# VectorE for one tile's output copies, the sums of w_out in one place, and sixteen small products of zeros: a change to a fused RWKV-6 and GELU-MLP kernel

## The chip, the cores and the metric

The kernel runs on one core of a Trainium2 chip. Its time is the device time in microseconds (us). Of a profiled execution there is also the span: the time from the core's first to its last instruction.

The engines are TensorE (matrix products; PE in the profile, PEld for its weight loads), VectorE (DVE), ScalarE (ACT), GpSimd (POOL) and SyncE (SP), which here only issues DMAs. A product of fp32 operands is executed as two passes, so the profile counts two matrix products for one in the code.

## The reference

The reference is a linear attention with a state (RWKV-6), followed by an MLP with exact GELU. All arrays are fp32 except the two weight matrices, which arrive as 64-bit floats.

```python
# r, k, v, w: (4, 8, 768, 48); u: (8, 48)
for t in range(S):
    cur = einsum('bhd,bhe->bhde', u[None] * kt, vt)
    y[:, :, t] = einsum('bhd,bhde->bhe', rt, state + cur)
    state = wt[:, :, :, None] * state + einsum('bhd,bhe->bhde', kt, vt)
x = y.transpose(0, 2, 1, 3).reshape(3072, 384)
h = x @ w_in                                   # w_in: (384, 2048)
g = 0.5 * h * (1.0 + erf(h / sqrt(2)))
out = g @ w_out                                # w_out: (2048, 384)
```

## The kernel before

The 3072 tokens are cut into eight tiles x = 0 to 7 of T = 384 tokens, two for each batch element. For each tile, `attention(x, unit)` computes the attention output, transposed, into the tile's `xT`, and `mlp(x)` computes the tile's rows of the output. Both are generators. The body of each `yield` is a piece of work, called a slot (attention) or a step (MLP) here. Each engine executes its instructions strictly in the order in which the generators emit them, so the order is written out by hand: the last loop of the kernel walks through the steps of `mlp(x - 1)` and, after chosen steps, emits slots of `attention(x)` and the first two slots of `attention(x + 1)`.

**The prelude.** A VectorE instruction fills `zeros` (bf16). `keep_warm(n)` issues n products of zeros of 512 columns into a PSUM tile that nobody reads (L194). Eight of them stand ahead of everything on TensorE, and two or three more stand after each slot of the first tile. The first tile's attention is done in two units of half the heads each, slot by slot. In the slots, TensorE makes products into the PSUM tile `d` (L406), VectorE scales r and k in place (L451) and copies the parts of `d` under a mask into `a_sb` (L461, L417). Slots that follow use transposes (L581), products of k and v (`kv_ps`, L607), the states (L622), and the products that give `y_ps` (L648, L689).

**The first MLP, `mlp(0)`.** It has steps 0 to 33. In steps 0 to 15, TensorE multiplies `xT` by w_in into `h_ps` (L886), and ScalarE applies GELU, the last 128 tokens going to `alone` (L889, L891). In steps 16 to 31 the products of the first 256 tokens with w_out are summed in two PSUM tiles `o_ps` (L974); at step 31 ScalarE copies both to SBUF (L979) and SP stores them (L794). Steps 32 and 33 are the two halves of the sum over the last 128 tokens (L900): the first goes to SBUF with a ScalarE copy (L990), the second is added to it by VectorE (L993). All of these sums and `h_ps` share two PSUM banks, tag "mm": a tile waits until the one two before it has been read.

Beside these steps, up to step 24, VectorE and ScalarE convert the weights from 64-bit floats (L295 to L314, `convert`), and the second tile's attention proceeds. Its last slot (at step 30) has the products L689, the ScalarE copy L715, six small DMAs out of it (L719, four on SP and two on ScalarE's queue) and six ScalarE copies into `xT` (L712).

**The sums of w_out, `w_sums`.** From the second tile on, the MLP replaces eight block products by seven, with sums and differences of blocks. The sums of w_out's blocks are made once: eight VectorE instructions of 128 x 768 elements (L739), one for each `next(more)`. In the kernel before, four are emitted at steps 30 to 33 of `mlp(0)`, and four at steps 9 to 12 of `mlp(1)`. `make_quarter_masks` issues nine small VectorE instructions (L246 to L260) and five GpSimd ones (L250, L255).

**Attention from the third tile on.** Slot one is four VectorE products (L356) and a transposing sum (L343). Slot two is the products of w (L375), more products and sums (L350, L379, L343). Then come rows laid out by ScalarE and VectorE (L502, L507, L508), the products L522 and L529 on TensorE, the updates of r and k (L536, L542, L545), the masked copies (L560, L567), and a block transpose of k (L481) whose off-diagonal blocks are moved by DMA (L476) and whose diagonal ones by ScalarE (L591). The products L607 need all these blocks. `place` and `place_next` list the steps after which slots are emitted.

Of the kernel before, what the change touches and what calls it, by code (L numbers as in the profile page):

```python
# [44 lines left out]
def kernel(  # L45
# [25 lines left out]
    nc = tc.nc  # L71
# [7 lines left out]
    NF = DF // 128  # L79
# [54 lines left out]
    def load(x, dma):  # L134

        if x >= NX:
            return
        loaded[x] = [None, None]
        for i in range(3):
            if i == 1:  # L140
                load_v(x, dma)
                yield
            t = bufs[x % 2 if i == 0 else 1]
            for j in range(3):
                a = i * ALL + j * ALL // 3
                dma.dma_start(out=t[:, a:a + ALL // 3], in_=rkw[x, :, a:a + ALL // 3])
                yield
# [33 lines left out]
    zeros = const.tile([128, BANK], BF16, name="zeros")  # L181
# [3 lines left out]

    nc.scalar.activation(out=zeros[:, 0:1], in_=zeros[:, 0:1], func=AF.Gelu)

    def keep_warm(n, elsewhere=False):
        if elsewhere:
            t = pd.tile([128, 2, BANK], F32, name="warm", tag="d")[:, 0]  # L190
        else:
            t = ps.tile([128, BANK], F32, name="warm", tag="mm", bufs=2)
        for _ in range(n):
            nc.tensor.matmul(t, lhsT=zeros[:, 0:128], rhs=zeros, start=True, stop=True)  # L194

    keep_warm(8)


    masks = {h: const.tile([128, C // 2], U8, name=f"mask{h}") for h in LEVELS[:-1]}
# [34 lines left out]
    for i, h in enumerate(QUARTERS):  # L234
        for a in range(3):
            w_q = (3 - a) * C // 4
            z = q_ints[1 if a == 0 else 2]
            o = i * C if a < 2 else i * C + C // 2
# [18 lines left out]
    def make_quarter_masks():  # L257
        make_fine()
        for (h, a), m_q in m_qs.items():
            nc.vector.tensor_tensor(out=quarter[h][a], in0=s_qs[h][:, 0:m_q.shape[1]], in1=m_q, op=ALU.is_equal)  # L260
# [22 lines left out]
    def convert():  # L283
        for _ in conversion():
            pass
# [446 lines left out]
    def w_sums():  # L732

        sums.extend(cv.tile([128, HF, HM], F32, name="t", tag="raw", bufs=AHEAD) for _ in range(4))
        s3_sb.append(cv.tile([128, HF, 128], F32, name="s3", tag="raw", bufs=AHEAD))
        for i, (x, y) in enumerate((((0, 1), (0, 0)), ((1, 1), 0), ((1, 1), (0, 1)), ((1, 0), 1))):
            for k in range(2):
                ks = slice(k * FG, (k + 1) * FG)
                nc.vector.tensor_sub(sums[i][:, ks], w_quarter(*x, k), sums[y][:, ks] if isinstance(y, int) else w_quarter(*y, k))  # L739
                yield  # L740
# [40 lines left out]
    def mlp(x):  # L781
# [8 lines left out]
        def block(a, b, j):  # L790
            return gs[2 * b + j // FG][:, j % FG, a * 128:(a + 1) * 128]

        def store(row0, o_sb, c0=0):
            nc.sync.dma_start(out=out[row0:row0 + 128, c0:c0 + o_sb.shape[1]], in_=o_sb)  # L794

        def new_sums(tag):
            return cv.tile([128, FG, 128], F32, name="s", tag=tag)
# [83 lines left out]
        for n, group in enumerate(() if final else (0, 2, 1, 3) if halves else range(4)):  # L881
            gs[group] = gp.tile([128, FG, T], F32, name="g")
            for f in range(group * FG, (group + 1) * FG):
                h_ps = ps.tile([128, BANK], F32, name="h_ps", tag="mm", bufs=2)[:, 0:T]
                for j in range(NJ):
                    nc.tensor.matmul(h_ps, lhsT=w_in_sb[:, f // FI, j, f % FI * 128:(f % FI + 1) * 128], rhs=xT[:, j, :],  # L886
                                     start=(j == 0), stop=(j == NJ - 1))
                t = T - 128 if waits else T
# [9 lines left out]
        def product(o, lhs, rhs, start=False):  # L898
            for j in range(HF):
                nc.tensor.matmul(o, lhsT=lhs(j), rhs=rhs(j), start=start and j == 0, stop=(j == HF - 1),  # L900
                                 skip_group_check=True)

        def of_sums(s):
            return lambda j: s[j // FG][:, j % FG, :]

        def of_t(i):
            return lambda j: sums[i][:, j, :]

        def of_blocks(a, b):
            return lambda j: block(a, b, j)  # L910
# [4 lines left out]
        def of_w(b, c):  # L915
            return lambda j: w_out_sb[:, b * HF + j, c * HM:(c + 1) * HM]

        def psum():
            return ps.tile([128, BANK], F32, name="o_ps", tag="mm", bufs=2)[:, 0:HM]

        def two_rows():
            return [wk.tile([128, DM], F32, name="o_sb", bufs=2) for _ in range(2)]
# [3 lines left out]
        if halves:  # L926
            o_sb = two_rows()
            p1, u2, u3 = (wk.tile([128, HM], F32, name=name, bufs=1) for name in ("p1", "u2", "u3"))
            o1, o2 = psum(), psum()
            product(o1, of_blocks(0, 0), of_w(0, 0), True)  # L930
            nc.scalar.copy(out=p1, in_=o1)  # L931
            yield
            product(o2, of_blocks(1, 1), of_t(3), True)
            nc.scalar.copy(out=o_sb[1][:, 0:HM], in_=o2)
            yield
            product(o1, of_blocks(0, 1), of_w(1, 0))
            nc.scalar.copy(out=o_sb[0][:, 0:HM], in_=o1)
            yield
            product(o2, of_sums(s2), of_t(1), True)
            nc.vector.tensor_add(u2, o2, p1)  # L940
            yield
            product(o1, of_sums(s1), of_t(0), True)
            nc.scalar.copy(out=o_sb[1][:, HM:], in_=o1)
            for k in range(2):

                nc.vector.tensor_sub(s2[k], gs[k + 2][:, :, 0:128], s2[k])
            yield
            product(o2, of_sums(s3), of_t(2))
            nc.vector.tensor_add(u3, o2, p1)
            for c in range(2):  # L950
                z = o_sb[1][:, c * HM:(c + 1) * HM]
                nc.vector.tensor_add(z, z, u3)
            store(row0 + 128, o_sb[1])
            if ends:
                s1 = [new_sums("f") for k in range(2)]
                for k in range(2):
                    nc.vector.tensor_add(s1[k], gs[k][:, :, 256:], gs[k + 2][:, :, 256:])
                    nc.vector.tensor_sub(s3[k], alone[:, k * FG:(k + 1) * FG], gs[k][:, :, 256:])
            yield
            product(o1, of_sums(s2), of_w(1, 1))  # L960
            nc.vector.tensor_add(o_sb[0][:, HM:], o1, u2)
            store(row0, o_sb[0])
            if ends:
                s2 = [new_sums("e") for k in range(2)]
                for k in range(2):
                    nc.vector.tensor_sub(s2[k], s1[k], alone[:, k * FG:(k + 1) * FG])
            yield

        else:

            o_ps = [ps.tile([128, BANK], F32, name="o_ps", tag="mm", bufs=2)[:, 0:DM] for _ in range(2)]
            for f in range(NF):
                for i, o in enumerate(o_ps):
                    nc.tensor.matmul(o, lhsT=block(i, f // HF, f % HF), rhs=w_out_sb[:, f, :], start=(f == 0), stop=(f == NF - 1))  # L974
                if f < NF - 1:
                    yield
            for i, o in enumerate(o_ps):
                o_sb = wk.tile([128, DM], F32, name="o_sb", bufs=2)
                nc.scalar.copy(out=o_sb, in_=o)  # L979
                store(row0 + i * 128, o_sb)  # L980
            yield


        if waits:
# [3 lines left out]
            o_sb = wk.tile([128, DM], F32, name="o_sb", bufs=2)  # L988
# [7 lines left out]
        elif ends:  # L996
            o_sb = two_rows()
# [69 lines left out]
    for x in range(1, NX):  # L1067

        place = [1, 3, 5, 7, 9, 11, 13, 15, 18, 20, 26, 30] if x == 1 else [1, 6, 8, 13, 15, 16, 18, 18, 20, 21]
        place_next = [31, 33] if x == 1 else [25, 27] if x % 2 == 0 else [21, 24]  # L1070
        loads = load(x + 1, nc.scalar if x > 1 else nc.sync)

        times = range(18, 28) if x == 1 else (2, 3, 4, 5, 17, 18, 19, 20, 21, 22)
        following = attention(x + 1, 0) if x + 1 < NX else iter(())
        for step, _ in enumerate(mlp(x - 1)):
            if x == 1 and step == 2 * NF - 2:

                make_quarter_masks()
                more = w_sums()

            if x == 1 or step > 8:
                next(more, None)
            if x == 1 and step in (0, 2, 4, 6, 8, 10, 12, 14, 15, 17, 18, 20, 22, 24):
                convert()
            if step in times:
                next(loads, None)
            while place and place[0] <= step:
                place.pop(0)
                next(slots, None)
            while place_next and place_next[0] <= step:  # L1090
                place_next.pop(0)
                next(following, None)
            if x == NX - 1:

                if step == 18:
                    more_h = h_sums()
                for _ in range({18: 1, 20: 1, 22: 2, 23: 1}.get(step, 0)):
                    next(more_h)
        for _ in slots:
            pass  # L1100
        slots = following
    for _ in mlp(NX - 1):
        pass
# [60 lines left out]
```

## Time and profile before

| What | Value |
|---|---|
| median of 11 runs | 611.49 us (609.44 to 613.98) |
| profiled execution | 612.44 us, its span 610.7 us |
| TensorE busy | 592.3 us (97%) in 7056 products |
| TensorE weight loads | 464.3 us (76%) |
| VectorE busy | 473.2 us (77%) in 909 instructions |
| ScalarE busy | 180.2 us (30%) |
| GpSimd busy | 8.4 us (1%) |
| mean granted TensorE clock | 0.994 |

The start of an instruction is given in us from the start of the span. "L" with a number is the line of the kernel before. A row of a timeline has the start, the time that the row covers, the engine, the line, the operation, the tiles written and read, their size, and how many instructions it merges; in brackets is the idle time of the engine ahead of it and what ended it. "issue" there means that the profile shows nothing that the engine waited for. The stages of this execution lie at 0 to 42 us (prelude), 42 to 130.17 (first MLP), and then, from the first `h_ps` product of each MLP to that of the next, at 130.17, 205.11, 270.39, 343.25, 408.53, 481.38 and 546.67.

### The profile page before, as it was taken

Reading aid. Unit: us, or ns where it says so; the run is one execution under the profiler, and the core shown is the slowest. Engines: PE = TensorE matmul, PEld = TensorE weight load, DVE = VectorE, ACT = ScalarE, POOL = GpSimd, SP = SyncE. Lnnn points to the kernel's source line nnn. Section 1 sums busy time; section 2 is a strip of 40 time slices with the busy share of each in tenths; the row PEclk is TensorE's granted clock in tenths of the full one; section 3 lists DMA queues with packets and bytes.
Section 4 is the critical chain, followed back from the end, with each engine's and each line's share of the span. In section 5 each row is a group of like instructions: output and inputs, shape, how many; then the busy total and the mean of one; then the engine's idle time right before and its main releaser. Section 6 shows DMA issues by size and latency. Waiting matters only on the chain.

```text
span 610.7 us, 16270 instructions
## 1 busy us (share of the span) xinstructions
PE 592.3 (97%) x7056; PEld 464.3 (76%) x7056; DVE 473.2 (77%) x909; ACT 180.2 (30%) x434; POOL 8.4 (1%) x24
## 2 busy tenths in 40 slices
PE   8889999899999999999999999999999999999997
PEld 4565666476689766986699766986699866999997
DVE  7887999958984988669884988769784988855632
ACT  2354567123212132223222132223222132224300
POOL 3100000000000000000000000000000000000000
PEclk9998999989999999999999999999999999999999
DMA  5667348013042121423042120423042000210000
GB/s 196 203 205 268 105 157 296 15 34 90 2 92 90 37 75 17 109 63 92 1 93 90 30 81 9 97 83 91 2 92 90 20 1 5 37 44 2 0 14 33
DMA packets 50711, 46.74 MB, mean 77 GB/s; under 512 B 31696, under 2 KB 36048, under 8 KB 50640
## 3 DMA queue, kind: packets, MB, share of 16 engines
q1 hardware_dynamic: 33296, 29.31, 15.6%
q10 hardware_dynamic: 17344, 16.39, 9.9%
q8 instruction: 56, 0.92, 0.6%
q14 instruction: 15, 0.12, 0.1%
HBM read 36.24 MB, written 4.72 MB: 67 GB/s over the span
## 4 chain that ended last, share of the span: by engine, by line
PE 85%; DVE 11%; issue 2%; ACT 1%; DMA 1%; SPq 0%; ACTq 0%; DVEq 0%
PE o_ps L900 32%; PE h_ps L886 29%; PE b L839 5%; PE d L529 4%; PE o_ps L974 3%; PE d L406 3%; PE kv_ps L607 2%; PE y_ps L689 2%; PE y_ps L648 2%; PE warm L194 2%; DVE rkw L451 1%; DVE a_sb L461 1%; DVE rkw L379 1%; PE d L522 1%; DVE kx L350 1%
## 5 line engine op out<-in xcount | busy, mean ns | idle before, releaser
L886 PE MATMUL h_ps<-xT,w_in_sb 128*128 128x384 f32 x672 | 224.7, 492 | 0.3 <-PE warm L194 0.3
L886 PEld LDWEIGHTS h_ps<-xT,w_in_sb 128*128 128x128 f32 x672 | 126.6, 191 | 85.6 <-issue 1.7
L889 ACT ACTIVATE g<-h_ps 128x256 f32<-128x256 f32 (+1 forms) x112 | 47.8, 429 | 171.6 <-PE h_ps L886 171.6
L900 PE MATMUL o_ps<-t,s 128*128 128x192 f32 x528 | 89.8, 328 | 0.0
L900 PEld LDWEIGHTS o_ps<-t,s 128*128 128x128 f32 x528 | 85.6, 190 | 0.7
L560 DVE COPY_PREDICATED a_sb<-quarter,d 128x384 f32<-128x384 uint8 (+2 forms) x108 | 45.1, 438 | 2.5
L900 PE MATMUL o_ps<-w_out_sb,g 128*128 128x192 f32 x224 | 38.8, 326 | 0.0
L900 PEld LDWEIGHTS o_ps<-w_out_sb,g 128*128 128x128 f32 x224 | 36.9, 190 | 1.8 <-ACT p L931 0.2
L622 DVE SCALAR_TENSOR_TENSOR st<-st,tot_sb,kv_ps 128x48 f32<-128x48 f32 x160 | 29.0, 258 | 4.2 <-PE kv_ps L607 4.1
L900 PE MATMUL o_ps<-w_out_sb,s 128*128 128x192 f32 x176 | 31.0, 330 | 0.0
L406 PEld LDWEIGHTS d<-rkw 64*64 64x64 f32 x1152 | 19.1, 136 | 15.1 <-DVE rkw L451 6.5
L900 PE MATMUL o_ps<-t,g 128*128 128x192 f32 x176 | 30.4, 326 | 0.0
L900 PEld LDWEIGHTS o_ps<-t,g 128*128 128x128 f32 x176 | 28.9, 190 | 0.0
L900 PEld LDWEIGHTS o_ps<-w_out_sb,s 128*128 128x128 f32 x176 | 28.6, 190 | 0.4
L406 PE MATMUL d<-rkw 64*64 64x64 f32 (+1 forms) x1152 | 21.8, 223 | 5.5 <-issue 2.5
L529 PEld LDWEIGHTS d<-kx,rkw 64*64 64x64 f32 x1152 | 24.3, 133 | 3.8 <-issue 1.6
L900 PE MATMUL o_ps<-w_out_sb,rkw 128*128 128x192 f32 x128 | 23.2, 344 | 4.0 <-ACT o_sb L979 4.0
L343 DVE TRANSPOSE_TENSOR_REDUCE rkw<-kx 128x48 f32<-128x1536 f32 (+3 forms) x24 | 26.8, 1155 | 0.2
L529 PE MATMUL d<-kx,rkw 64*64 64x96 f32 x1152 | 26.5, 245 | 0.3 <-DVE kx L508 0.3
L900 PEld LDWEIGHTS o_ps<-w_out_sb,rkw 128*128 128x128 f32 x128 | 22.5, 202 | 4.6 <-ACT o_sb L979 4.6
L379 DVE TENSOR_TENSOR rkw<-rkw 128x384 f32<-128x384 f32 (+2 forms) x24 | 23.5, 1002 | 0.4
L502 ACT COPY kx<-rkw 128x384 f32<-128x384 f32 x36 | 16.1, 509 | 26.3 <-PE d L529 15.4
(146 smaller groups left out, 734.9 us busy)
## 6 DMA issues: line engine op xcount, KB each, us to landing
rkw<-in_rkw_dram ACTq DMA_DIRECT2D x45, 256.0 KB, 2.8
raw<-in_w_out_dram SPq DMA_DIRECT2D x8, 768.0 KB, 4.3
raw<-in_w_in_dram SPq DMA_DIRECT2D x5, 768.0 KB, 6.5
out_dram<-o_sb SPq DMA_DIRECT2D x20, 192.0 KB, 1.9
v_in<-in_v_dram ACTq DMA_DIRECT2D x5, 584.0 KB, 3.8
raw<-in_w_in_dram SPq DMA_DIRECT2D x9, 256.0 KB, 3.8
rkw<-in_rkw_dram SPq DMA_DIRECT2D x8, 288.0 KB, 3.5
rkw<-in_rkw_dram SPq DMA_DIRECT2D x9, 256.0 KB, 7.4
```

The lines of the kernel that those rows point to most:

```text
L343: nc.vector.tensor_reduce(out=fine_sb[:, e, 0:n].rearrange("p a n -> p (a n)"), in_=kx[:, o:o + n * n_m].rearrange("p (m j) -> p m j", j=3 ...
L379: nc.vector.tensor_mul(z, z, by)
L406: nc.tensor.matmul(d[half[p], g, n * width:(n + 1) * width], lhsT=kc[half[g], b, i, p], rhs=right(half[g], b, i, p), start=True, stop=True)
L502: nc.scalar.copy(out=z, in_=r4[:, :, :, f, :])
L529: nc.tensor.matmul(d[half[p], g, i * 3 * C // 2:(i + 1) * 3 * C // 2], lhsT=kc[half[g], (n + i) // NI, (n + i) % NI, p], rhs=rx[half[g], 2 ...
L560: nc.vector.copy_predicated(out=an[:, :, :, :, (a + 1) * h:], mask=mask.to_broadcast(data.shape), data=data)
L622: nc.vector.scalar_tensor_tensor(out=stq[:, q, c], in0=stq[:, q, c - 1] if c else b4[:, q, NC - 1], scalar=totq[:, q, c:c + 1], in1=kvs[q ...
L839: nc.tensor.matmul(o, lhsT=lhsT, rhs=rhs, start=start and i == 0, stop=(i == len(factors) - 1), skip_group_check=True)
L886: nc.tensor.matmul(h_ps, lhsT=w_in_sb[:, f // FI, j, f % FI * 128:(f % FI + 1) * 128], rhs=xT[:, j, :], start=(j == 0), stop=(j == NJ - 1))
L889: nc.scalar.activation(out=gs[group][:, f % FG, 0:t], in_=h_ps[:, 0:t], func=AF.Gelu)
L900: nc.tensor.matmul(o, lhsT=lhs(j), rhs=rhs(j), start=start and j == 0, stop=(j == HF - 1), skip_group_check=True)
L974: nc.tensor.matmul(o, lhsT=block(i, f // HF, f % HF), rhs=w_out_sb[:, f, :], start=(f == 0), stop=(f == NF - 1))
```

## The change

There are four edits. In the prelude, sixteen products of zeros with 64 columns follow the first eight products. At the end of step 31 of the first MLP, VectorE and no longer ScalarE copies the two `o_ps` tiles. The masks and the first of the sums of w_out are emitted after step 28 and no longer after step 30, and after steps 32 and 33 two sums are emitted each, so that all eight lie in the first MLP. Slot one of the third tile's attention is emitted after step 32, and no longer after step 31. The order on VectorE from the masks on is then: three sums, the two copies, three sums, slot one, the addition at L993, two sums, slot two.

```diff
+    warm_of = []
+
     def keep_warm(n, elsewhere=False):
         if elsewhere:
             t = pd.tile([128, 2, BANK], F32, name="warm", tag="d")[:, 0]
         else:
             t = ps.tile([128, BANK], F32, name="warm", tag="mm", bufs=2)
+        warm_of[:] = [t]
         for _ in range(n):
             nc.tensor.matmul(t, lhsT=zeros[:, 0:128], rhs=zeros, start=True, stop=True)
 
     keep_warm(8)
+
+    for _ in range(16):
+        nc.tensor.matmul(warm_of[0][:, 0:64], lhsT=zeros[:, 0:128], rhs=zeros[:, 0:64], start=True, stop=True)
...
             for i, o in enumerate(o_ps):
                 o_sb = wk.tile([128, DM], F32, name="o_sb", bufs=2)
-                nc.scalar.copy(out=o_sb, in_=o)
+                nc.vector.tensor_copy(out=o_sb, in_=o)
                 store(row0 + i * 128, o_sb)
...
-        place_next = [31, 33] if x == 1 else [25, 27] if x % 2 == 0 else [21, 24]
+        place_next = [32, 33] if x == 1 else [25, 27] if x % 2 == 0 else [21, 24]
...
         for step, _ in enumerate(mlp(x - 1)):
-            if x == 1 and step == 2 * NF - 2:
+            if x == 1 and step == 2 * NF - 4:
 
                 make_quarter_masks()
                 more = w_sums()
 
-            if x == 1 or step > 8:
+            for _ in range(2 if x == 1 and step > 31 else 1):
                 next(more, None)
```

## The prediction

> **What bounds the kernel now.** I read the chain that ended last first, then the costliest groups, then TensorE's and VectorE's timelines at each gap. From the page:
>
> ```profile
> PEclk9998999989999999999999999999999999999999
> ...
> PE 85%; DVE 11%; issue 2%; ACT 1%; DMA 1%; SPq 0%; ACTq 0%; DVEq 0%
> ...
> L900 PE MATMUL o_ps<-w_out_sb,rkw 128*128 128x192 f32 x128 | 23.2, 344 | 4.0 <-ACT o_sb L979 4.0
> ```
>
> TensorE carries the path, so a change is worth the TensorE idle time it removes or adds, and the cold time with it. The largest gap, 4.0 us, ends with ScalarE's copies at L979. The timeline of that place:
>
> ```profile
> 117.62 1.56 PE L974 MATMUL o_ps<-w_out_sb,g 128*128 128x384 f32 x4
> ...
> 119.73 2.90 ACT L712 COPY xT<-y_ps 48x384 f32<-48x384 f32 x6 [1.50 <-issue]
> ...
> 122.66 0.86 ACT L979 COPY o_sb<-o_ps 128x384 f32<-128x384 f32 x2
> ...
> 123.19 7.15 PE L900 MATMUL o_ps<-w_out_sb,rkw 128*128 128x192 f32 x32 [4.01 <-ACT o_sb L979]
> ```
>
> TensorE ends its sums at 119.18, but ScalarE first issues two DMAs and makes six xT copies. The following 32 products start 6.98 us ahead of the next row (130.17); the same 32 in the third tile take 5.20 (265.19 to 270.39). The stage table has why, and an earlier cold place (columns: length, busy time of PE, PEld, DVE, ACT, POOL, clock, DMA):
>
> ```profile
> 51.00:54.00 3.00, 3.00 (x10) 1.69 (x7) 2.92 (x5) 0.00 (x0) 0.00 (x0) 0.67 0.90 276
> ...
> 124.00:126.00 2.00, 2.00 (x8) 2.00 (x7) 0.00 (x0) 0.00 (x0) 0.00 (x0) 0.50 0.54 197
> ```
>
> The clock records give half speed from 52.00 to 55.42 and from 123.68 to 127.10. The first follows a gap with no releaser:
>
> ```profile
> 47.73 1.58 PE L406 MATMUL d<-rkw 64*64 64x32 f32 x91
> ...
> 50.80 0.31 PE L406 MATMUL d<-rkw 64*64 64x32 f32 x5 [1.49 <-issue]
> ...
> 51.04 5.83 PE L886 MATMUL h_ps<-xT,w_in_sb 128*128 128x384 f32 x12
> ...
> 58.49 1.76 DVE L451 TENSOR_TENSOR rkw<-rkw 128x1536 f32<-128x1536 f32 x1 [3.51 <-PE d L406]
> ```
>
> VectorE waits 3.51 us at L451, so gap and cold stretch are on the path. Then the second MLP:
>
> ```profile
> 130.43 0.36 DVE L993 TENSOR_TENSOR o_sb<-o_ps,rkw 128x192 f32<-128x192 f32 x1 [7.32 <-PE o_ps L900]
> ...
> 131.57 0.95 DVE L375 TENSOR_TENSOR tot_sb<-rkw 128x768 f32<-128x768 f32 x1
> ...
> 147.96 0.96 DVE L508 TENSOR_TENSOR kx<-kx,tot_sb 128x768 f32<-128x768 f32 x1 [0.40 <-ACT kx L502]
> ...
> 149.07 2.21 PE L529 MATMUL d<-kx,rkw 64*64 64x96 f32 x96 [0.32 <-DVE kx L508]
> ...
> 162.26 1.82 DVE L739 TENSOR_TENSOR t<-w_out_sb,t 128x768 f32<-128x768 f32 x2
> ...
> 176.70 1.69 PE L607 MATMUL kv_ps<-v_in,rkw 64*64 64x48 f32 x92 [1.10 <-DMA rkw<-kx]
> ```
>
> VectorE's chain from L375 (131.57) to L508's end (148.92) is as long as TensorE's work beside it: L529 waits 0.32. Four sums of w_out (two rows, 160.54 to 163.99) delay the block moves, and L607 waits 1.10 for a move. Last, the prelude:
>
> ```profile
> 2.28 4.88 PE L194 MATMUL warm<-zeros 128*128 128x512 bf16 x11 [2.28 <-ACT zeros L186]
> ...
> 7.09 1.16 PE L406 MATMUL d<-rkw 64*64 64x64 f32 x48
> ...
> 9.99 0.96 DVE L451 TENSOR_TENSOR rkw<-rkw 128x768 f32<-128x768 f32 x1 [1.07 <-PE d L406]
> ```
>
> TensorE goes from zeros to L406 without a gap although ScalarE had its data at 6.13; VectorE waits 1.07 for it.
>
> [...] both cold stretches last 3.41 us and lie 21 windows apart. A window with 1.49 us idle gave a cold one; the one with 1.10 (L607) did not. [...] counted in TensorE's queue, the gaps at 23.5, 27.5, 36.4 and 49.1 sit exactly at instructions 960, 1216, 1728 and 2240, multiples of 256 plus 192, and each ends 2.2 to 2.6 us after an instruction packet starts. [...] the 384-element copy at L712 takes 0.56 on VectorE, that at L979 0.48 on ScalarE.
>
> **The change part by part.** About 0.3% (1.8 us) is what a measurement can tell from no change.
>
> *1. Copies on VectorE.* VectorE's new order: masks, three sums, two copies, three sums, the slot of L356 and L343, the add L993, two sums, then L375. A sum takes 0.87 (115.72 to 117.45 for two). Three end at 118.3; o_ps 0 is done at about 118.5 (the record of L974's second pass ends there), so copy one is 118.6 to 119.15, copy two 119.2 to 119.8. TensorE loses nearly none of the 4.01, and without idle no cold stretch: 32 products end at 119.2 + 5.2 = 124.4 instead of 130.17. xT is ready (copies end 122.6, the small DMAs land by about 123). ScalarE's L990 follows at 122.7, while both stores behind the moves on SP start earlier; neither holds anything.
> But VectorE is late next. Three sums: 119.8 to 122.4. Slot: 4.74 (117.45 to 122.19), to 127.15; it was in the shadow of ScalarE before. L993: to 127.4. Behind it waits the second h_ps bank, which TensorE wants at 124.4 + 1.95 (17.58/9) = 126.35: 1.1 us idle. Two more sums: L375 starts at 129.2 against 131.57, 2.4 earlier. L508 keeps its distance and ends at 146.5; L529 starts at 146.7, not 149.07: **-2.4**. TensorE is there at 127.5 + 8 x 1.95 + 1.0 (L522) = 144.1, so it idles 2.6 us, above the 1.49 that gave a cold window, in nearly every phase. A cold window costs 3.41/2 = 1.7, less if part of it falls on the idle: **+1.5** (0 to 1.7).
>
> *2. No sums in the second MLP.* From the first h_ps it takes 74.94 (130.17 to 205.11), the fourth, without sums, 72.86 (270.39 to 343.25). Of the 2.08, 0.39 lie ahead of L529 and are in part 1; the rest goes: **-1.7** (-1.3 to -1.7). VectorE's L542 then waits for L529, as there, and L481 comes early enough for the moves.
>
> *3. Masks two steps earlier, slot one later.* VectorE's order shows the masks where they were, after the fences. POOL's five instructions ran at 15.7 to 18.8, waiting only for L451: nothing. The slot's shift is counted in part 1; no DMA or SP entry moves with it.
>
> *4. Sixteen products of zeros.* No row has them. Each has a weight load (record at this clock 0.15) [...]. [...] the clock is granted at 7.63, three products of zeros then take 0.75, and L406 starts at about 8.1 instead of 7.09, but warm: 0.93, not 1.16. L451 moves by **+0.7** (0.2 if the clock comes early and the DMA is the limit, 1.6 at 0.15 each). Below zero is excluded for this work itself, as it stands ahead of L406 on the path; nothing later up to 119 has slack for it.
>
> *5. They shift the blocks.* 32 instructions more put every block border 32 instructions earlier in the code. In the prelude the borders stay inside runs of L406: about 0 (-0.4 to +0.5). The one at 49.1 is different. The packet for it came at 48.35, seven microseconds after the previous border (41.13). [...] Either way the block should be there: **-1.5**, and the cold stretch at 52.0 goes: **-1.7** in this run.
>
> Sum against the profiled execution, 612.44 (span 610.7 and 1.7 around it): -2.4 + 1.5 - 1.7 + 0.7 - 1.5 - 1.7 = -5.1, so **607.3**. That execution is 0.95 above the median 611.49; I take this to be the cold stretch at 52.0, which other phases lack and the changed kernel would lack always, so 607.3 stands for the median too.
>
> **The rivals.** (a) *The fetch stall stays.* What asks for a block isn't shown, and the DMA share is 1.06 there. Then 3.2 less: 610.5 in a run like the profiled, 609.5 from the median. 0.25. (b) *No cold window at L529*, if the idle splits over two windows or VectorE is quicker: 605.8. 0.10. (c) *VectorE too late for the copies*: sums ahead slower than 0.87, TensorE idles on, and only part 2 and a piece of part 1 remain: 611. 0.06. (d) *Slower: the small products keep the clock down.* [...] each further cold window costs 1.7 on top of 16 x 0.15 = 2.4. [...] Without the gain of part 5, parts 1 and 2 bring 2.6; above 2.6 + 1.8 = 4.4 it is slower. Two windows: 5.8, 614.7. 0.04.
>
> **How the numbers follow.** The forecast has 0.55. Faster by over 0.3% (under 609.7): nearly all of it, (b), and somewhat over half of (a): 0.79. Within: the rest of (a), most of (c): 0.16. Slower: (d) and a little of (c): 0.05. The range goes from (b) with a cheap prelude, 604.9, to (a) with a dear one, 610.3.
>
> **What would show it.** After: L900 behind L974 without a gap and in 5.2 us; an idle of about 1.1 at the second h_ps and 2.6 at L529, both released by VectorE; a cold stretch right after the latter; L607 without a wait; L406 of the second tile unbroken, no cold stretch near 52; the first L406 0.5 to 1.5 later. It is wrong if the time is above 610.3, if L900 still waits for o_sb by over 1 us, or if L529 starts less than 1.5 us earlier relative to the first h_ps of the first MLP.

## The result and the profile after

| What | Before | After |
|---|---|---|
| median | 610.94 us of 47 runs (608.68 to 613.98) | 607.17 us of 12 runs (604.67 to 608.36) |
| span of the profiled execution | 610.7 us | 605.4 us |
| mean granted clock in it | 0.994 | 0.997 |

The ratio of the times is 0.9936, with an interval of 0.9922 to 0.995: faster by 0.5 to 0.8%. Line numbers of the changed kernel are 6 higher from `masks` on (L406 is L412, L529 is L535). The page of the changed kernel, first the clock by slices, then the shares of the chain that ended last, then two groups of instructions:

```profile
PEclk9999999998999999999999999999999999999999
...
PE 89%; DVE 8%; issue 2%; ACT 0%; DVEq 0%
...
L892 PE MATMUL h_ps<-xT,w_in_sb 128*128 128x384 f32 x672 | 223.5, 489 | 0.8 <-DVE o_sb L999 0.8
...
L535 PE MATMUL d<-kx,rkw 64*64 64x96 f32 x1152 | 27.9, 252 | 2.3 <-DVE kx L514 2.3
```

Before, two slices of the clock were low, now one is. ScalarE's share of the chain is 0%, from 1%, and the group that idled 4.0 us for ScalarE's copies has left the list. In its place stand two waits for VectorE, 0.8 and 2.3 us. TensorE's timeline of the same execution shows the places of the prediction (start, time covered, engine, line, operation, tiles, size, count, idle time ahead and its releaser):

```profile
5.68 0.93 PE L202 MATMUL warm<-zeros 128*128 128x64 bf16 x16
...
7.18 0.93 PE L412 MATMUL d<-rkw 64*64 64x64 f32 x48
...
37.34 0.69 PE L613 MATMUL kv_ps<-v_in,kx 64*64 64x48 f32 x33 [1.30 <-issue]
...
48.12 1.60 PE L412 MATMUL d<-rkw 64*64 64x32 f32 x96
...
53.71 1.63 PE L412 MATMUL d<-kx,rkw 64*64 64x64 f32 x96
...
114.54 1.56 PE L980 MATMUL o_ps<-w_out_sb,g 128*128 128x384 f32 x4
...
116.11 5.47 PE L906 MATMUL o_ps<-w_out_sb,rkw 128*128 128x192 f32 x32
...
124.35 15.75 PE L892 MATMUL h_ps<-xT,w_in_sb 128*128 128x384 f32 x48 [0.84 <-DVE o_sb L999]
...
143.42 3.56 PE L535 MATMUL d<-kx,rkw 64*64 64x96 f32 x96 [2.33 <-DVE kx L514]
...
170.80 1.61 PE L613 MATMUL kv_ps<-v_in,rkw 64*64 64x48 f32 x96
```

The 96 products at 48.12 are unbroken, where a gap of 1.49 had cut the last five off. L906 follows L980 with no gap, and its 32 products end at 121.41, where `h_ps` follows; before, that was at 130.17. Of these 8.8 us, 3.1 had come up by the end of L980 (116.1 instead of 119.18), and 5.7 come from the idle time and the cold stretch behind it. From 121.41 on, part is given back: 0.84 at the second `h_ps` bank, 2.33 at L535, and L535 itself takes 3.56 us instead of 2.21. The stage table has the reason (columns: length, busy time of PE, PEld, DVE, ACT, POOL, clock, DMA share, GB/s):

```profile
141.00:144.00 3.00, 0.67 (x18) 0.61 (x20) 2.46 (x4) 2.10 (x5) 0.00 (x0) 0.81 0.00 0
144.00:147.00 3.00, 3.00 (x92) 2.88 (x84) 0.74 (x1) 0.00 (x0) 0.00 (x0) 0.62 0.03 5
```

TensorE is busy for 0.67 of three microseconds, and the clock is then at half speed from 142.85 to 146.27. The third MLP's `h_ps` comes at 199.12 instead of 205.11, and the span is shorter by 5.3.

### The profile page after: what moved, and what is told of

Read it like the earlier page. It is cut to its first block, busy times and chain, and to the rows that moved or that the text cites. A ratio compares the mean times of both kernels' runs of the same rounds, so it can differ in the third digit from the quotient of the medians.

```text
span 605.4 us, 16301 instructions
## 1 busy us (share of the span) xinstructions
PE 590.3 (98%) x7072; PEld 463.2 (77%) x7072; DVE 474.6 (78%) x911; ACT 179.1 (30%) x432; POOL 8.4 (1%) x24
## 4 chain that ended last, share of the span: by engine, by line
PE 89%; DVE 8%; issue 2%; ACT 0%; DVEq 0%
PE o_ps L906 33%; PE h_ps L892 32%; PE b L845 5%; PE d L535 4%; PE o_ps L980 4%; PE d L412 3%; PE kv_ps L613 2%; PE y_ps L695 2%; PE y_ps L654 2%; PE warm L197 2%; DVE rkw L457 1%; DVE a_sb L467 1%; DVE rkw L385 1%; PE d L528 1%; DVE kx L356 1%
## 5 line engine op out<-in xcount | busy, mean ns | idle before, releaser
L906 PE MATMUL o_ps<-t,s 128*128 128x192 f32 x528 | 89.8, 328 | 0.0
L906 PEld LDWEIGHTS o_ps<-t,s 128*128 128x128 f32 x528 | 85.6, 190 | 0.7
L906 PE MATMUL o_ps<-w_out_sb,g 128*128 128x192 f32 x224 | 38.9, 327 | 0.0
L906 PEld LDWEIGHTS o_ps<-w_out_sb,g 128*128 128x128 f32 x224 | 36.8, 190 | 2.0 <-ACT p L937 0.4
L906 PE MATMUL o_ps<-w_out_sb,s 128*128 128x192 f32 x176 | 31.0, 330 | 0.0
L906 PE MATMUL o_ps<-t,g 128*128 128x192 f32 x176 | 30.4, 326 | 0.0
L535 PE MATMUL d<-kx,rkw 64*64 64x96 f32 x1152 | 27.9, 252 | 2.3 <-DVE kx L514 2.3
L535 PEld LDWEIGHTS d<-kx,rkw 64*64 64x64 f32 x1152 | 25.6, 139 | 5.8 <-ACT g L895 2.4
L906 PEld LDWEIGHTS o_ps<-t,g 128*128 128x128 f32 x176 | 28.9, 190 | 0.0
L906 PEld LDWEIGHTS o_ps<-w_out_sb,s 128*128 128x128 f32 x176 | 28.6, 190 | 0.4
L412 PEld LDWEIGHTS d<-rkw 64*64 64x64 f32 x1152 | 18.7, 134 | 12.6 <-DVE rkw L457 6.1
L548 DVE TENSOR_TENSOR rkw<-rkw,tot_sb 128x768 f32<-128x768 f32 x12 | 11.5, 958 | 18.4 <-PE d L535 18.4
L508 ACT COPY kx<-rkw 128x384 f32<-128x384 f32 x36 | 16.0, 508 | 29.8 <-PE d L535 16.8
L412 PE MATMUL d<-rkw 64*64 64x64 f32 (+1 forms) x1152 | 21.3, 221 | 3.6 <-DVE rkw L457 2.3
L718 ACT COPY xT<-y_ps 48x384 f32<-48x384 f32 x42 | 19.9, 473 | 14.2 <-issue 11.4
```

The lines of the kernel that those rows point to most:

```text
L412: nc.tensor.matmul(d[half[p], g, n * width:(n + 1) * width], lhsT=kc[half[g], b, i, p], rhs=right(half[g], b, i, p), start=True, stop=True)
L535: nc.tensor.matmul(d[half[p], g, i * 3 * C // 2:(i + 1) * 3 * C // 2], lhsT=kc[half[g], (n + i) // NI, (n + i) % NI, p], rhs=rx[half[g], 2 ...
L718: copy(out=xT[s, pair, :].rearrange("p (i c t) -> p c i t", c=2, t=C), in_=y[s])
```

## The experiments

Each kernel was timed beside the kernel before, on the same chip. Two questions were open: which part brings the gain, and by what the sixteen products act. My theory was the prediction's sum: copies and sums bring some 2.6 us, and the products remove a stall by moving the blocks of instructions (a block here is 256 instructions of TensorE's queue: the gaps at 960, 1216, 1728 and 2240 in the profile of before lie whole multiples of 256 apart). The rivals were that the products act by warming the clock or not at all, that the sums bring nothing, and that the idle time at L529 lies in the copies' place and not in that of the sums.

### One part at a time

The changed kernel without the sixteen products, the kernel before with only them, with only the copies, and with only the sums (these four ran on one chip):

```diff
 # e1_no16, on the kernel after
-    for _ in range(16):
-        nc.tensor.matmul(warm_of[0][:, 0:64], lhsT=zeros[:, 0:128], rhs=zeros[:, 0:64], start=True, stop=True)
 # e2_only16, on the kernel before
+    for _ in range(16):
+        nc.tensor.matmul(warm_of[0][:, 0:64], lhsT=zeros[:, 0:128], rhs=zeros[:, 0:64], start=True, stop=True)
 # e3_copies, on the kernel before
-                nc.scalar.copy(out=o_sb, in_=o)
+                nc.vector.tensor_copy(out=o_sb, in_=o)
 # e4_sums, on the kernel before
-            if x == 1 and step == 2 * NF - 2:
+            if x == 1 and step == 2 * NF - 4:
-            if x == 1 or step > 8:
+            for _ in range(2 if x == 1 and step > 31 else 1):
```

> The changed kernel without the sixteen small products. Theory (they shift the instruction blocks): the gap of about 1.5 us in the second tile's L406 comes back in the trace, at instruction 2240 of TensorE's queue, with a cold stretch behind it in some executions; the time is about 1.5 to 2.5 above the changed kernel's 607.2, so 608.7 to 609.7, ratio to before 0.996 to 0.998. Rival (the small products only cost their own time, and the gain is all from the copies and sums): no gap, and 606.5 to 607.2. Both theories have VectorE's idle of TensorE at L529 near 2.3.

> The kernel before with the sixteen small products and nothing else. Theory: the gap at about 49 us goes, the cold stretch at 52 with it, other borders in the prelude cost 0.3 more: 1.5 to 2.3 faster than before, ratio 0.996 to 0.9975. Rival: the products cost 0.1 to 0.8, ratio 1.000 to 1.0015. The 4.0 idle at L900 and the 1.1 at L607 stay in both.

> The kernel before with the two o_ps copies on VectorE and nothing else: two sums stay ahead of slot one, one behind it, one behind L993, four in the second MLP. Theory (VectorE's chain to L508 sets the time from here to L529): L375 starts 4.1 earlier than before, L529 too, TensorE idles about 1.7 there with a cold window in about half of the executions; the wait of 1.1 at L607 stays. 3 to 4 faster, ratio 0.9935 to 0.995. Rival (the copies need the sums out of the second MLP to bring anything): at most 1.5 faster, ratio over 0.9975.

> The kernel before with all eight sums in the first MLP and nothing else: copies on ScalarE, slot one after step 31. Theory: two more sums behind L993 put L375 and L529 0.9 later relative to the first h_ps, the wait at L607 and the rest of the second MLP's surplus (1.7) goes: 0.8 faster, ratio 0.998 to 0.9995. Rival (the sums in the second MLP were hidden): 0.9 slower, ratio 1.0015.

| Kernel | median, us | ratio to before (interval) |
|---|---|---|
| e1_no16 | 607.9 | 0.995 (0.9936 to 0.9964) |
| e2_only16 | 609.01 | 0.9978 (0.9964 to 0.9991) |
| e3_copies | 606.31 | 0.9933 (0.9912 to 0.9954) |
| e4_sums | 610.53 | 1.0008 (0.9987 to 1.0028) |

e4_sums leaves slot one after step 31. The ratios of e2_only16, e3_copies and e4_sums miss their forecasts by 0.0013 at most, with intervals that reach into them; that of e4_sums takes in the rival's 1.0015 as well. e1_no16 was forecast at 608.7 to 609.7 and came out at 607.9, between theory and rival.

**The products of zeros.** Without them the gap in the second tile's L406 is back; TensorE's timeline of e1_no16:

```profile
46.34 1.58 PE L410 MATMUL d<-rkw 64*64 64x32 f32 x91
...
48.86 0.31 PE L410 MATMUL d<-rkw 64*64 64x32 f32 x5 [0.94 <-issue]
```

With only them it is gone, as the timeline of e2_only16 shows:

```profile
47.39 1.60 PE L412 MATMUL d<-rkw 64*64 64x32 f32 x96
```

The gap lies again at instruction 2240 of TensorE's queue. The last instruction packet ahead of it starts at 46.62 in e1_no16 and at 41.44 in e2_only16. No cold stretch followed the gap in this execution of e1_no16. By their mean clocks, 12 of its 21 executions had two cold stretches or more (0.994 or less; the profile of before has 0.994 with two, that of the changed kernel 0.997 with one), and 3 of the 18 of the changed kernel (with e10_after); where they fell isn't recorded. The gain of e2_only16 is 1.4 us (610.42 to 609.01), by the interval 0.5 to 2.2. The prediction's +0.7 - 3.2, reckoned from the median as it was there (0.95 less), is 1.55, but the terms don't hold one by one (parts 4 and 5 below).

**The copies** alone are as fast as the whole change. **The sums** alone bring nothing that these runs can tell. e4_sums removes the wait at L607, as it was meant to, and pays at L529 (its timeline):

```profile
148.53 3.76 PE L529 MATMUL d<-kx,rkw 64*64 64x96 f32 x96 [1.21 <-DVE kx L508]
```

The idle time is 1.21 instead of 0.32, and a cold stretch from 148.96 makes L529 take 3.76. I had not foreseen a cold stretch there.

e3_copies has a shorter wait at L607 and no cold stretch at L529. In its timeline the gap in L406 stays (1.76), L529 idles 1.50 at full clock, and L607 still waits:

```profile
50.25 0.31 PE L406 MATMUL d<-rkw 64*64 64x32 f32 x5 [1.76 <-issue]
...
144.24 2.21 PE L529 MATMUL d<-kx,rkw 64*64 64x96 f32 x96 [1.50 <-DVE kx L508]
...
172.05 1.69 PE L607 MATMUL kv_ps<-v_in,rkw 64*64 64x48 f32 x92 [0.74 <-DMA rkw<-kx]
```

### What the sixteen products act by

The same instruction count placed where TensorE waits for VectorE anyway, and the reverse: more work of the same kind with only four instructions more. On the chip with them ran the copies together with the sixteen.

```diff
 # e5_shadow16, on the kernel before: in the first tile's loop over slots, after keep_warm
+            if slot == 3 and unit is units[0]:
+                for _ in range(16):
+                    nc.tensor.matmul(warm_of[0][:, 0:64], lhsT=zeros[:, 0:128], rhs=zeros[:, 0:64], start=True, stop=True)
 # e6_warm10, on the kernel before
-    keep_warm(8)
+    keep_warm(10)
 # e7_copies16: the edits of e2_only16 and e3_copies together
```

> The kernel before with the sixteen small products, but placed where TensorE waits 0.7 us for VectorE (behind the two products of zeros that follow the fifth run of L406, at about 15.8), not ahead of the first L406. Theory (the number of instructions ahead of the second tile's L406 counts, not where their time falls): the gap at 48 to 50 us is absent as with the products at the start, the instruction packet comes near 42 and not near 47; ratio to before 0.9965 to 0.9985. Rival (the products at the start help the clock[...]): no gain here, the gap stays, ratio 0.999 to 1.001.

> The kernel before with two more 512-column products of zeros at the start: as much TensorE time as the sixteen small ones (0.85 at half clock against 0.76), but 4 instructions instead of 32. Theory (instructions count): the gap of 1 to 2 us in the second tile's L406 stays, the prelude is 0.2 to 0.8 later; ratio 1.000 to 1.0015. Rival (more work at the start helps by the clock): gap smaller or gone, ratio under 0.9985.

> The kernel before with the two copies on VectorE and the sixteen small products; sums and slot one where they were. Theory (the two edits act in different stages and add; moving the sums brings nothing on balance): 0.9933 x 0.9978 = 0.991, 605.0, below the changed kernel's 0.9936; TensorE idles about 1.5 at L529 and 0.7 at L607. Rival (the sums out of the second MLP carry a part of the changed kernel's gain of over 1 us): 0.9935 or more.

e5_shadow16: 608.32 us, 0.9973 (0.996 to 0.9986). e6_warm10: 611.23, 1.001 (0.9998 to 1.0021). e7_copies16: 605.11, 0.9918 (0.9892 to 0.9943). All three came as the theory had it, though the interval of e7_copies16 takes in the rival's 0.9935 as well; its profile idles 1.49 at L535 and 0.74 at L613. In TensorE's timeline of e5_shadow16 the products fill a wait for VectorE, of which 0.25 is left of 0.71, and the run of L406 is whole:

```profile
15.51 0.63 PE L1051 MATMUL warm<-zeros 128*128 128x64 bf16 x16
...
48.42 1.60 PE L409 MATMUL d<-rkw 64*64 64x32 f32 x96
```

In e6_warm10 the gap stays, 0.99 from 48.42. The DMA view's line for the queue of instructions shows where the packet came early. It has one packet between 40 and 44.5 us in the changed kernel, and none from there to 48.8 (columns: packets, MB, share of the DMA engines' time):

```profile
q8 instruction: 1, 0.02, 2.2%
```

In e6_warm10 it is the reverse, one packet between 45 and 48.8:

```profile
q8 instruction: 1, 0.02, 1.7%
```

So the number of instructions acts, and not the work or the warmth. In all eight profiles with the sixteen products, 32 instructions, the packet starts at 40.9 to 43.9, which is 0.5 to 1.9 us ahead of the first `h_ps`. In all six with fewer instructions, it starts at 46.3 to 48.4, 4.2 to 4.9 us behind the first `h_ps`.

### GpSimd in the place of VectorE

If VectorE's queue is what is late at L529, the sums could go to the idle GpSimd.

```diff
 # e8_poolsums, on e7_copies16 (in w_sums)
-                nc.vector.tensor_sub(sums[i][:, ks], ...)
+                nc.gpsimd.tensor_sub(sums[i][:, ks], ...)
```

> As the run with copies on VectorE and sixteen small products, but the eight sums of w_out on GpSimd, which is idle. Theory (the wait at L529 and the wait at L607 both come from VectorE's queue, the sums stand in it): L375 starts at about 2 us after the first h_ps of the second MLP or sooner, TensorE's idle at L529 is under 0.5 with no cold stretch, L607 waits under 0.2; 2 to 3.5 faster than with the sums on VectorE, ratio to before 0.986 to 0.989. Rival (GpSimd is too slow [...]): the products with the sums wait for GpSimd, or VectorE's L350 to L379 take over 5% longer; no gain or a loss, ratio 0.991 or more.

612.61 us, 1.0038 (1.0027 to 1.0049): slower than the kernel before, and on the rival's side. A sum takes 1.83 us on GpSimd, which would not matter, but VectorE's masks are slow beside it. The timelines of both engines in e8_poolsums:

```profile
113.47 0.21 DVE L252 TENSOR_TENSOR fine_mask<-p,u 128x64 uint8<-128x64 int32 x1
113.56 1.84 POOL L745 TENSOR_TENSOR t<-w_out_sb,t 128x768 f32<-128x768 f32 x1 [7.42 <-DVE fence L666]
113.60 1.88 DVE L253 TENSOR_TENSOR later<-u,p 128x64 uint8<-128x64 int32 x1
...
117.23 5.66 DVE L266 TENSOR_TENSOR quarter<-p,u 128x48 uint8<-128x48 int32 x6
...
122.81 1.01 DVE L985 COPY o_sb<-o_ps 128x384 f32<-128x384 f32 x2
```

The mask at L253 takes 1.88 us beside a sum, where it takes 0.22 in the profile of before (L247 there); L254 takes 1.79, and the six at L266 take 5.66, where they take 0.69 in the changed kernel. The last sums on GpSimd end at 122.55. The copies, which stand behind the masks on VectorE, come at 122.81, TensorE idles 5.33 at L906, and 6.83 us of half clock follow from 121.39. Why the masks take so long beside the sums isn't shown. L535 and L613 don't wait in the second MLP, as the theory had it, but its first `h_ps` comes 7.65 us behind the start of the last 32 products and not 5.3, which gives VectorE time; so this run tells little on that.

### Where the sums stand in VectorE's order

Then the sums stayed on VectorE, but at places where TensorE doesn't wait for it: three ahead of the copies, none between the copies and L508, three between the quarter updates, where VectorE waits for the products L529, and the last two, whose result is read last, after steps 19 and 20 of the second MLP. The last two pairs of sums change places for that. Beside it ran the changed kernel and e7_copies16 again, and the changed kernel with half as many small products.

```diff
 # e9_spread, on e7_copies16
-        for i, (x, y) in enumerate((...)):
+        for i in (0, 1, 3, 2):
+            x, y = plan[i]
...
-            if x == 1 and step == 2 * NF - 2:
+            if x == 1 and step == 2 * NF - 4:
...
-            if x == 1 or step > 8:
-                next(more, None)
+            if of_w_sums and (x == 1 and step < 2 * NF - 1 or x == 2 and step in (19, 20)):
+                next(of_w_sums[0], None)
 # in the quarters of the third tile, after the multiply at L536
+                if x == 2:
+                    for _ in range(1 if last else 2):
+                        next(of_w_sums[0])
 # e10_after: the changed kernel. e11_copies16: e7_copies16
 # e12_n8, on the kernel after
-    for _ in range(16):
+    for _ in range(8):
```

> Copies on VectorE and the sixteen small products; of the sums of w_out three stand ahead of the copies, where VectorE waits for TensorE anyway, none between the copies and L508, two and one in the waits of VectorE for the two L529 (ahead of L542), and the last two, of the block that is needed last, after steps 19 and 20 of the second MLP. Theory (what costs at L529 and L607 is the place of each sum in VectorE's queue): L375 starts 2.6 earlier relative to the first h_ps of the second MLP than with sums in slot one's way, TensorE idles under 0.3 at L529 and L607, no cold stretch at either; 602.5 to 603.5, ratio to before 0.987 to 0.989. Rival (the second MLP is limited there by something else, as ScalarE's rows L502 or the moves): idle over 0.8 at one of the two places, ratio 0.991 or more.

> The changed kernel, on the same chip as the other runs of this call. Its ratio to before was 0.9936. If moving the sums and slot one costs about 0.8 to 1.0 us, as the pairs of runs so far say (0.995 against 0.9933 without the small products, 0.9936 against 0.9918 with them), it is slower here than the kernel with copies and small products alone by 0.001 to 0.002; if the pairs differ by chance, by 0.0005 or less.

> Copies on VectorE and the sixteen small products, sums and slot one where they were, again and on the same chip as the changed kernel: see there. Ratio 0.9915 to 0.9925 if the sums' place costs, 0.9936 if not.

> The changed kernel with eight small products (16 instructions) in place of sixteen. Theory (the request for the block with instruction 2240 waits for TensorE to pass a certain instruction behind border 1984; with 32 instructions fewer ahead it is one of the products of zeros or h_ps at 42 to 48, with 32 more one of L689 ahead of them): with 16 the packet comes between, at 42 to 46, and the gap is 0 to 0.9; time within 0.7 of the changed kernel. Rival (any shift removes the gap, by chance of the DMA traffic): packet as late as without or as early as with sixteen.

| Kernel | median, us | ratio to before (interval) | start of last 32 products to the third MLP's `h_ps`, us |
|---|---|---|---|
| e10_after | 606.87 | 0.9938 (0.9915 to 0.9962) | 115.91 to 199.14: 83.23 |
| e11_copies16 | 604.0 | 0.9881 (0.9857 to 0.9905) | 117.76 to 199.04: 81.28 |
| e9_spread | 601.25 | 0.9843 (0.9818 to 0.9868) | 114.74 to 192.90: 78.16 |
| e12_n8 | 607.14 | 0.9939 (0.9916 to 0.9961) | not used |

e9_spread is faster than was forecast (0.987 to 0.989), with four executions only. e10_after and e11_copies16 differ by 2.9 us, where 0.6 to 1.2 were expected. The two other such pairs differ by 1.1 (0.9936 and 0.9918, on different chips) and 1.6 (e1_no16 and e3_copies), with intervals that overlap. The direction is the same in all three; the size stays open between these values.

e11_copies16 has no idle time at the second `h_ps` and no cold stretch, but two waits (its TensorE timeline):

```profile
143.40 2.21 PE L535 MATMUL d<-kx,rkw 64*64 64x96 f32 x96 [1.50 <-DVE kx L514]
...
170.63 1.69 PE L613 MATMUL kv_ps<-v_in,rkw 64*64 64x48 f32 x92 [0.90 <-DMA rkw<-kx]
```

e9_spread has none of them. Its TensorE timeline:

```profile
114.74 5.47 PE L912 MATMUL o_ps<-w_out_sb,rkw 128*128 128x192 f32 x32
120.05 17.58 PE L898 MATMUL h_ps<-xT,w_in_sb 128*128 128x384 f32 x54
...
138.55 2.21 PE L536 MATMUL d<-kx,rkw 64*64 64x96 f32 x96
...
164.57 1.61 PE L617 MATMUL kv_ps<-v_in,rkw 64*64 64x48 f32 x96
```

and VectorE's, with the first of slot two and the sums that follow it:

```profile
120.58 0.95 DVE L382 TENSOR_TENSOR tot_sb<-rkw 128x768 f32<-128x768 f32 x1
...
139.34 1.82 DVE L751 TENSOR_TENSOR t<-w_out_sb,t 128x768 f32<-128x768 f32 x2
...
151.52 0.94 DVE L751 TENSOR_TENSOR t<-w_out_sb,t 128x768 f32<-128x768 f32 x1
```

Slot two starts 5.84 us behind the start of the last 32 products. In the changed kernel it starts 9.83 behind them, as its VectorE timeline shows:

```profile
115.49 1.20 DVE L985 COPY o_sb<-o_ps 128x384 f32<-128x384 f32 x2 [0.17 <-PE o_ps L980]
...
123.98 0.32 DVE L999 TENSOR_TENSOR o_sb<-o_ps,rkw 128x192 f32<-128x192 f32 x1
...
125.94 0.95 DVE L381 TENSOR_TENSOR tot_sb<-rkw 128x768 f32<-128x768 f32 x1
```

The three stretches of the table can be added up. Against e9_spread, e10_after idles 0.84 and 2.37, and a cold stretch from 143.06 costs 1.6 (half of the 3.21 in which TensorE worked): 4.8 of a difference of 5.07. e11_copies16 idles 1.50 and 0.90: 2.4 of 3.12. Between e9_spread and e11_copies16 only the places and the order of the sums differ, and the place of the masks, which move two steps up with them. So the idle times at `h_ps`, L535 and L613 all come from where the sums stand in VectorE's queue, and e9_spread, without them, beats both kernels: about 9.6 us under the one before (610.89), 5.6 under the changed one.

e12_n8, with 16 instructions more than without the products, has the gap (1.02, from 47.67) and a packet as late as without them (46.34). A packet at 42 to 46 was forecast, so the theory on what the packet waits for has no support; the time, that of e10_after, was as forecast. In its profile the first `h_ps` comes at 42.17 instead of 43.89. One pair of executions doesn't settle whether fewer products make the prelude shorter: in e7_copies16 and e11_copies16, the same program, that point lies at 44.36 and 45.75. Part 5 below takes all profiles together.

## Why the prediction was right, point by point

*1. Copies on VectorE.* Right at every step. The copies end at 116.69, the first early enough for L906 to start without a gap, and its 32 products take 5.30 (5.2 forecast). VectorE's chain has the forecast length: L375 starts 9.83 behind the start of these products (10.0 forecast), L529 27.31 (27.5). From the end of L974 to L529 it is 27.32 instead of 29.89, so the term is -2.6 (-2.4 forecast). The idle times are 0.84 at the second `h_ps` and 2.33 at L529, where 1.1 and 2.6 were forecast, since TensorE also gets there 0.1 to 0.25 later than reckoned. The cold stretch at L529 came in all four profiles with this order (after, e1_no16, e10_after, e12_n8), and 11 of the changed kernel's 12 executions have a mean clock under 1, so rival (b) fell. Its price was 1.4 in the first of them, with 0.57 of the 3.41 on idle time; +1.5 was forecast. Rival (c) fell too: three sums were done before the products were.

*2. No sums in the second MLP.* The wait at L607 is gone, as forecast. From L529 to the third `h_ps` the changed kernel takes 55.70 instead of 56.04: -1.7 and the cold stretch's +1.4. The term was right. But it wasn't necessary to take the sums out of this MLP: e9_spread, without a cold stretch, takes 54.35 (138.55 to 192.90), also -1.7, with five sums in it, at places where TensorE doesn't wait for VectorE.

But the prediction did not ask whether parts 2 and 3 had better been left out. With them, five sums stand between the copies and slot two, without them three, and I had charged all of that delay to part 1. e11_copies16 leaves out just parts 2 and 3 of what e10_after has (604.0 and 606.87, intervals apart). It saves 0.84 at `h_ps`, 0.87 at L535 and 1.6 of cold time, 3.3 in all, and gives up part 2's 1.7. That is 1.6 net; the traces show 1.95 up to the third `h_ps`, and the medians 2.9, of which the rest isn't explained.

*3. Masks and slot.* Nothing beyond the above was seen. Neither the earlier masks nor the later slot one was tried apart.

*4. Sixteen products.* Forecast +0.7 (0.2 to 1.6), with the first L406 0.5 to 1.5 later. The first L412 came at 7.18 instead of 7.09, but +0.1 is not their price. The clock was granted at 6.32, not 7.63, so L412 ran in 0.93 instead of 1.16, and when the grant comes differs between executions. e3_copies has no such products and the grant at 6.35. Its TensorE timeline:

```profile
6.75 0.93 PE L406 MATMUL d<-rkw 64*64 64x64 f32 x48
```

By that the sixteen cost 0.43, which is 0.3 less than forecast. They took 0.76 us. Ahead of the grant they start 0.053 apart, an eighth of the 0.42 of the products of 512 columns in front of them (eight from 2.29 to 5.68). The forecast had them twice as slow; that was an estimate that no trace had shown, and the measurement decides. e6_warm10 gives a bound for such work: two products of 512 columns cost 0.001 (-0.0002 to 0.0021) of the time, 0.6 us, 1.3 at most. Rival (d) fell: no cold window followed the products.

*5. Blocks.* The gap went and with it the cold stretch at 52, as forecast, by the cause that was forecast, the shift of the blocks; rival (a) fell. That the block would be there in time was an estimate; why an earlier border brings an earlier packet isn't shown. The prelude's share was taken as about 0 (-0.4 to +0.5), with all borders inside runs of L406. But one stood in L607 before, with a wait of 0.41 from 36.62; now it falls where TensorE waits 1.30 at L613 (36.04 to 37.34), 0.48 are new at L695 (41.34), and other waits are shorter.

The first `h_ps` came only 0.17 later than in the profile of before, whose clock was granted last of the six profiles without the sixteen. All profiles together say more. In those six it comes at 42.2 to 43.7 (mean 42.7), in the eight with the sixteen at 42.8 to 45.8 (mean 43.9). From there to the end of the first MLP's L974 it takes 72.0 to 72.2 with the sixteen (but 75.2 in e8_poolsums), 73.2 to 73.3 in the three profiles with the gap alone, and 75.5 to 75.7 in the three with gap and cold stretch. So the block is worth 1.2 us, or 3.5 with the cold stretch. The sixteen seem to cost about 1 in the prelude, of which part 4 explains 0.43; the ranges overlap, and this is not tested apart. It fits the runs. e2_only16 and e5_shadow16 gain 0.2 to 0.3% on the kernel before. On top of the other parts, the ratios 0.9936 (after) and 0.995 (e1_no16) differ by 0.9 us, with intervals that overlap, and e12_n8 is as fast with the gap. What the sixteen are worth in the changed kernel is small and stays open.

The sum was -5.1, and the span shrank by 5.3, but in part by luck. At the third `h_ps` it stands at -6.0: 0.3 because part 4 was reckoned too dear, 0.3 because the clock was granted earlier, 0.3 behind L974. From there to the end 0.7 is lost again: the MLP that starts at 264.41 takes 73.71 us instead of 72.86. Most of it comes up at the first products of L613 (309.1 to 309.8), with a wait of 0.30 without a releaser. The same MLP takes 73.5 to 73.8 in e3_copies, e9_spread, e10_after and e12_n8 too. All of these have the copies on VectorE, but so have e1_no16, e7_copies16, e8_poolsums and e11_copies16, where it takes 72.85; the cause is open.

The step to the median was wrong. I had put the 0.95 us of the profiled execution above the median down to its second cold stretch. But 81 of the 129 later executions of the kernel before have a mean clock of 0.994 or less, which is two cold stretches or more (two take 3.41 of 611 us, 0.006), so the median isn't free of them. Among the profiles, what stands out in that one is the late grant and the late first `h_ps` (43.69, against 42.2 to 42.9 in the five others without the sixteen). From median to median the change brings 3.8 us, where 607.3 meant 4.2 from the median known then and 5.1 from the profiled execution. That 607.17 lies within 0.2 us of it is in part luck.

## What to carry to other kernels

When work moves to an engine that has room on average, read what that engine must deliver next, and count everything queued between: here the copies alone brought 4.1 us, and the changed kernel, with five sums that could wait between the copies and slot two, is 5.6 slower than the one that has the same copies and products and these sums in VectorE's waits. Put such filler into the new engine's own waits, and last what is read last. Where a gap has no releaser and falls at the same count of instructions, change the count by some and see whether it moves, before it is put down to the work.

## What the runs showed of the hardware that was not expected

- The length of an idle time alone didn't tell which clock followed. The clock records of before change at 7.63, 52.00, 55.42, 123.68 and 127.10 (13, 1, 20 and 1 times 3.413 us apart), those of the changed kernel at 6.32, 142.85 and 146.27 (40 times and once), and the cold stretches of e4_sums start 71.68 and 27.30 apart (21 and 8 times). So stretches of 3.41 us, here called windows, can be placed by these changes. In e4_sums the window from 145.55 to 148.96 held 1.21 of idle time, and half clock followed; the one from 32.92 to 36.33 in the same execution held 1.51, and full clock followed, as it did behind 1.50 in e11_copies16 (141.45 to 144.86, placed by its grant at 8.33). Beside the idle time, the first had mostly `h_ps` and L522, 16 products of 48 columns in 1.06 us, the second L607 and L648, the third L535; what decided isn't shown.
- Half clock lasted two windows in a row, 6.83 us, in e6_warm10 and e8_poolsums, behind 4.0 and 5.3 us without work. The length of the idle time alone didn't tell that either: in e6_warm10 3.3 of the 4.0 lay in the first window and 0.67 in the second, in e5_shadow16 3.4 and 0.58, and there full clock came back after one window.
- The instruction packet came some 5 us earlier (42.5 instead of 47.2 on average) when the code was shifted by 32 instructions: a packet ahead of the first `h_ps` left no gap, one 4.2 us or more behind it left 0.9 to 1.8 us in each of the six profiles. A shift by 16 didn't move it (46.34 in e12_n8). What starts the packet isn't shown.
